# A linear-attention and gated-MLP kernel: issuing from one fixed table instead of by priorities, and short elementwise sums kept in PSUM

## The chip, the cores and the metric

The kernel runs on one core of a Trainium2 chip. TensorE (PE) multiplies matrices into PSUM, of which the kernel uses eight banks; VectorE (DVE), ScalarE (ACT) and GpSimd (POOL) do the elementwise work, POOL on SBUF alone here; SyncE (SP) issues the transfers. Each engine works through its own queue in order and waits on semaphores. The metric is the device time in microseconds (us), the median of the runs.

## What is computed

Three layers follow each other, here as the reference writes them:

```python
for t in range(S):                                   # B=4, H=8, S=768, D=48
    cur = einsum('bhd,bhe->bhde', u * k[t], v[t])
    y[t] = einsum('bhd,bhde->bhe', r[t], state + cur)
    state = w[t][..., None] * state + einsum('bhd,bhe->bhde', k[t], v[t])
x = y, heads side by side                            # 4 x 768 x 384
h = gelu_tanh(x @ w_in); u, v = split(h)             # 512 + 512 columns
v = layernorm(v) * g_ln
v_s = einsum('ts,bsd->btd', w_sg, v) + b_sg
x = x + (u * v_s) @ w_out
gate = sigmoid(causal 5-tap convolution of x over t, one filter per column)
out = (gate * (x @ w_val)) @ w_out2
```

All is float32. Weights of the dense layers arrive as 64-bit numbers and are turned into float32 on ACT and DVE.

## The kernel before

**Attention.** The recurrence runs in chunks of 64 tokens. A unit is one batch, one segment of 256 tokens and one pair of heads: 4 x 3 x 4 = 48 units, 12 to a batch. A unit is a chain of small steps, each a function named by one letter: F and E (L271, L276: prefix products of the decay, DVE scans), L (L280, POOL), K (L283), D (L287, ACT), t (L297, PE transposes), s (L303, PE), k (L307, ACT), m (L311, DVE reads the scores), v (L316, ACT), B (L328 and L333, PE: the products of keys and values), o (L338 ACT and L342 POOL), d (L347, ACT reads what B wrote), a (L353, DVE scan over the chunk states), S and p (L358, L363, ACT), C (L372, PE: the outputs) and y (L377, DVE adds what C wrote to y). One call of the generator `attention(b)` is a tick: it issues different stages of three neighbouring units.

**Dense work.** Tokens of a batch are taken in two halves of 384. Every dense product is made of three passes over fp32r halves (hi and lo of each operand, `PASS` L485), so each operand is first split: ACT copies the hi half, DVE or POOL subtracts to get lo. The steps: xT (L478 PE transposes of y, L481 ACT, L482 DVE), hv (L499 PE, then `ln`: L503 ACT gelu, L505 to L511 DVE with L510 POOL, L514 ACT, L515 POOL), u (PE L522 into `ups`, L535 ACT gelu into `ut`), x2_init (L548 POOL: x again as a sum of its halves), vs (PE L522 into `vps`, 18 matmuls; L562 DVE adds the bias into the SBUF tile `gt`), gated (L573 POOL gt = gt * ut, L575 ACT hi, L576 DVE lo into `gl`), wo (L586 PE, three banks c0 to c2 over four d; then for each bank L597 DVE adds x into the SBUF tile x2, L598 ACT hi and L599 POOL lo of `x2hl`), conv (L615 ACT, L618 four DVE operations, L620 ACT tanh), val (PE L522 into `val`; L631 DVE multiplies by the gate into SBUF, L633 ACT hi, L634 DVE lo into `ml`), out (L644 PE, L650 ACT, L652 the transfer out).

**Order.** Batch 0's attention runs first, together with the decoding of weights (`to_f32`, L150 to L157). Then `phase(b)` walks a list of words (`ORDER0`, `ORDER`, `LAST`), which mixes the dense steps of batch b with ticks T of the attention of batch b+1. That is the program order. The order on each engine is then set by a scheduler: it takes the ready operation of the best priority by its own estimate of times, and the table `LEAD` (L112) moves the priority of each kind of step forward or back. Decoding of w_o1 is held behind batch 0's layer norm with `issue_after` (L743).

**PSUM.** `psA` has three banks (tags a0: t and s, a1: B, a2: C and from batch 1 on xT), `psD` two banks, shared by hv, ups, vps and val (and xT in batch 0), and `psC` three (c0 to c2), which wo, conv and out use in turn, and odd units of batch 0.

Of the kernel before, what the change touches and what calls it, by code (L numbers as in the profile page):

```python
# [25 lines left out]
C = 64  # L26
# [24 lines left out]

@with_exitstack
def tile_kernel(ctx, tc, pk, sv_, rk_, v_, u_, misc_, w_in, w_sgT, b_sg, w_o1, w_val,
                cw, w_o2, ident_, out):
    nc = tc.nc
    pe, act, dve, pool, sp = nc.tensor, nc.scalar, nc.vector, nc.gpsimd, nc.sync
# [10 lines left out]
    psD = ctx.enter_context(tc.tile_pool(name="psD", bufs=2, space=bass.MemoryType.PSUM))  # L67
# [39 lines left out]
    def every(name):  # L107
# [4 lines left out]
    LEAD = {  # L112
# [3 lines left out]
        112, "gate": -97, "wo": -19, "woo": 94, "cv": -371, "val": 38, "out": 2, "outo":  # L116
        203, "dec": 6, "spl": 66, "bon": 100, "du": 177, "dw": -92}

    @contextmanager
    def lead(kind):  # L120
        at = tc.cur_priority
        tc.cur_priority = at - LEAD.get(kind, 0)
        yield
        tc.cur_priority += LEAD.get(kind, 0)

    def leading(kind, f):
        def g(*args):
            with lead(kind):
                return f(*args)
        return g  # L130


    def stage(srcs, ring, tag, words):
# [3 lines left out]
        for src in srcs:  # L137
            n = src.shape[1] * (1 if src.dtype == F32 else 2)
            sp.dma_start(out=big[:, at:at + n], in_=src.bitcast(I32))
# [4 lines left out]
    def to_f32(bits, plain, t):  # L144
# [4 lines left out]
        with lead("dec"):  # L149
# [11 lines left out]
    def split(t, hi, lo):  # L161
        with lead("spl"):
            act.activation(out=hi, in_=t, func=AF.Copy)
            pool.tensor_tensor(out=lo, in0=t, in1=hi.bitcast(F32), op=ALU.subtract)
# [33 lines left out]
    def sg_step(hf, kk):  # L198
# [4 lines left out]
        sp.dma_start(out=t, in_=w_sgT[kk * 128:(kk + 1) * 128, hf * HALF:(hf + 1) * HALF])  # L203
# [9 lines left out]
    def load_nat(b, s):  # L213
        t = r2.tile([128, NT, DM], F32, tag="v", name="v")
        sp.dma_start(out=t, in_=v_[b, s * SEG:(s + 1) * SEG, :].rearrange("(j p) f -> p j f", p=128))
        vt[b, s] = t

    def load_rk(i):
        t = buf("rk", i, i // KS).rearrange("p (two f) -> p two f", two=2)
        sp.dma_start(out=t, in_=rk_[i // KS, i % KS * 128:(i % KS + 1) * 128, :, :])  # L220

    def bonus(b, i):

        s, j = divmod(i, NT)
        with lead("bon"):
# [13 lines left out]
    def load_unit(n):  # L239
        b, s, p = units[n]  # L240
        sp.dma_start(out=buf("pk", n), in_=pk[b, p, s])

    def load_sv(n):
        b, s, p = units[n]
        sp.dma_start(out=buf("sv", n), in_=sv_[b, p, s])

    def unit(n):
# [4 lines left out]
        kh, kn = buf("kh", n), buf("kn", n)  # L252
# [7 lines left out]
        F, E, d1e = buf("F", n), buf("E", n), buf("D1E", n)  # L260
# [62 lines left out]
        def kv():  # L323
            t["b"] = ps(1, n, [128, 512])
# [40 lines left out]
        def tokens():  # L365
            t["c"] = ps(2, n, [128, 512])
# [472 lines left out]
```

## Time and profile before

| | before |
|---|---|
| time, median of 3 runs | 558.68 us (556.5 to 559.03) |
| span of the profiled execution | 554.3 us |
| around the span | 4.4 us, taken as the median less the span |
| PE busy | 520.3 us (94%) |
| DVE busy | 417.0 us (75%) |
| ACT busy | 296.2 us (53%) |
| POOL busy | 267.5 us (48%) |
| mean granted TensorE clock | 0.954 |

The span is the profiled execution's own time from its first instruction to its last; the times include what lies around it. A row of the trace gives an engine, the source line, the tiles as out<-in, a count, busy time and mean duration; "idle before" is time in which the engine sat still before those instructions, with what released it. PE overlaps its matmuls, so the spacing of their starts, as the chain of work shows it, is what a matmul costs there.

### The profile page before, as it was taken

Reading aid. Unit: us, or ns where it says so; the run is one execution under the profiler, and the core shown is the slowest. Engines: PE = TensorE matmul, PEld = TensorE weight load, DVE = VectorE, ACT = ScalarE, POOL = GpSimd, SP = SyncE. Lnnn points to the kernel's source line nnn. Section 1 sums busy time; section 2 is a strip of 40 time slices with the busy share of each in tenths; the row PEclk is TensorE's granted clock in tenths of the full one; section 3 lists DMA queues with packets and bytes.
Section 4 is the critical chain, followed back from the end, with each engine's and each line's share of the span. In section 5 each row is a group of like instructions: output and inputs, shape, how many; then the busy total and the mean of one; then the engine's idle time right before and its main releaser. Section 6 shows DMA issues by size and latency. Waiting matters only on the chain.

```text
span 554.3 us, 10705 instructions
## 1 busy us (share of the span) xinstructions
PE 520.3 (94%) x4060; PEld 448.4 (81%) x4060; DVE 417.0 (75%) x823; ACT 296.2 (53%) x695; POOL 267.5 (48%) x282
## 2 busy tenths in 40 slices
PE   8978688979999999898999999999999999999995
PEld 4666566868988887787988888789989887999985
DVE  6999999899697769985299669965498349324673
ACT  4676856655475745743285746643484636323233
POOL 7477856674844246764154126861163125523430
PEclk9598788896999999999999999999999999999999
DMA  8961513424314343342115342232122100100002
GB/s 302 388 246 44 164 66 103 133 83 158 86 43 138 108 144 100 100 128 90 41 38 178 124 122 72 59 121 80 44 54 91 58 16 1 43 1 0 1 0 86
DMA packets 27075, 53.42 MB, mean 96 GB/s; under 512 B 3089, under 2 KB 17169, under 8 KB 27025
## 3 DMA queue, kind: packets, MB, share of 16 engines
q1 hardware_dynamic: 27024, 52.75, 29.4%
q8 instruction: 32, 0.52, 0.4%
q14 instruction: 19, 0.15, 0.1%
HBM read 48.02 MB, written 4.72 MB: 95 GB/s over the span
## 4 chain that ended last, share of the span: by engine, by line
PE 40%; DVE 16%; issue 3%; DMA 2%; POOL 1%; ACT 1%; POOLq 0%; SPq 0%; ACTq 0%; DVEq 0%
PE vps L522 12%; PE c L586 6%; PE ups L522 6%; PE o L644 4%; DVE cvp L618 4%; PE val L522 3%; PE a L372 3%; PE hv L499 2%; PE a L303 2%; PE a L328 2%; DVE cv L618 1%; PE a L297 1%; DVE SD L353 1%; DVE rk L229 1%; DMA rk<-in_rk_dram 1%
## 5 line engine op out<-in xcount | busy, mean ns | idle before, releaser
L522 PE MATMUL vps<-wsg,vnt 128*128 128x384 f32 x576 | 113.1, 341 | 0.0
L522 PEld LDWEIGHTS vps<-wsg,vnt 128*128 128x128 f32 x576 | 101.1, 190 | 1.0
L573 POOL TENSOR_TENSOR gt<-gt,ut 128x384 f32<-128x384 f32 x32 | 33.8, 1057 | 98.7 <-DVE gt L562 80.5
L499 PE MATMUL hv<-win,x 128*128 128x512 f32 x216 | 65.2, 431 | 3.7 <-DVE cv L631 2.2
L586 PE MATMUL c<-gl,late 128*128 128x384 f32 x288 | 62.6, 345 | 0.0
L522 PE MATMUL ups<-x,win 128*128 128x384 f32 x288 | 59.8, 350 | 1.5 <-DVE gt L562 1.5
L358 ACT ACTIVATE SE<-SD 64x192 f32<-64x192 f32 x80 | 45.1, 564 | 23.1 <-DVE SD L353 13.9
L522 PEld LDWEIGHTS ups<-x,win 128*128 128x128 f32 x288 | 51.4, 192 | 3.0 <-DVE gt L562 1.9
L586 PEld LDWEIGHTS c<-gl,late 128*128 128x128 f32 x288 | 50.2, 189 | 2.2
L499 PEld LDWEIGHTS hv<-win,x 128*128 128x128 f32 x216 | 41.4, 202 | 12.8 <-DVE cv L631 2.6
L280 POOL TENSOR_TENSOR L<-pk,E 128x256 f32<-128x256 f32 x38 | 30.9, 814 | 41.1 <-PE a L372 32.9
L618 DVE SCALAR_TENSOR_TENSOR cvp<-x,cw_col,cvp 128x384 f32<-128x384 f32 x84 | 48.7, 612 | 0.4 <-ACT cvp L615 0.2
L271 DVE TENSOR_TENSOR_SCAN F<-pk,D1F 128x260 f32<-128x260 f32 x40 | 35.3, 884 | 16.5 <-DMA pk<-in_pk_dram 12.3
L353 DVE TENSOR_TENSOR_SCAN SD<-SD,SD 128x288 f32<-128x288 f32 x48 | 43.4, 903 | 4.6 <-ACT SD L347 4.2
L522 PE MATMUL val<-x2hl,late 128*128 128x384 f32 x216 | 44.2, 344 | 2.2 <-ACT vg L503 1.8
L644 PE MATMUL o<-late,ml 128*128 128x384 f32 x216 | 43.9, 342 | 0.7 <-DVE ml L634 0.7
L316 ACT ACTIVATE vcd<-v 64x192 f32<-64x192 f32 x84 | 30.2, 359 | 26.8 <-PE a L328 25.8
L515 POOL TENSOR_TENSOR vnt<-vg,vnt 128x512 fp32r<-128x512 f32 x24 | 34.2, 1426 | 17.9 <-ACT vnt L514 15.3
L576 DVE TENSOR_TENSOR gl<-gt,gl 128x384 fp32r<-128x384 f32 x32 | 20.0, 624 | 29.9 <-ACT gl L575 29.7
L522 PEld LDWEIGHTS val<-x2hl,late 128*128 128x128 f32 x216 | 37.3, 188 | 5.3 <-ACT vg L503 2.7
L575 ACT ACTIVATE gl<-gt 128x384 fp32r<-128x384 f32 x32 | 16.7, 523 | 42.9 <-POOL gt L573 38.2
L644 PEld LDWEIGHTS o<-late,ml 128*128 128x128 f32 x216 | 37.5, 187 | 2.4 <-DVE ml L634 1.0
(154 smaller groups left out, 1102.8 us busy)
## 6 DMA issues: line engine op xcount, KB each, us to landing
pk<-in_pk_dram SPq DMA_DIRECT2D x40, 386.5 KB, 3.4
sv<-in_sv_dram SPq DMA_DIRECT2D x39, 192.0 KB, 2.4
v<-in_v_dram SPq DMA_DIRECT2D x12, 384.0 KB, 3.3
out_dram<-ot SPq DMA_DIRECT2D x24, 192.0 KB, 1.9
rk<-in_rk_dram SPq DMA_DIRECT2D x12, 384.0 KB, 3.1
bits<-in_w_in_dram SPq DMA_DIRECT2D x6, 512.0 KB, 6.8
room_l<-in_pk_dram SPq DMA_DIRECT2D x7, 386.5 KB, 7.1
bits<-in_w_o_dram SPq DMA_DIRECT2D x7, 384.0 KB, 5.3
```

What stands on the lines that cost most here:

```text
L271: dve.tensor_tensor_scan(out=F[:, NW:0:-1], data0=w[:, NW:0:-1], data1=D1F[:, NW:0:-1], initial=0.0, op0=ALU.mult, op1=ALU.add)
L280: pool.tensor_tensor(out=ch(L[:, 0, :]), in0=ch(r), in1=e3[:, :, 0:C], op=ALU.mult)
L316: act.activation(out=vcd[half[c2], :, c2, :], in_=vt[b, s][half[c2], :, 2 * p * D:(2 * p + 2) * D], func=AF.Copy)
L353: dve.tensor_tensor_scan(out=SD1, data0=SD1, data1=SD0, initial=0.0, op0=ALU.add, op1=ALU.mult)
L358: act.activation(out=S[half[hh], :, hh, :], func=AF.Copy, in_=d1[half[hh], :, 1:NC + 1].rearrange("p e c -> p c e"))
L499: pe.matmul(out=ps, lhsT=x[:, a, kk, j * 128:(j + 1) * 128], rhs=win[:, w, kk, DV:2 * DV], start=(z == 0), stop=(z == nmm - 1))
L515: pool.tensor_tensor(out=vnt[b][:, 1, i, :], in0=vg, in1=hi.bitcast(F32), op=ALU.subtract)]
L522: pe.matmul(out=ps, lhsT=lhs(a, kk), rhs=rhs(w, kk), start=(z == 0), stop=(z == nk * 3 - 1))
L573: pool.tensor_tensor(out=t, in0=t, in1=ut.pop((b, hf, d)), op=ALU.mult)
L586: pe.matmul(out=acc[0][f], lhsT=late["wo1"][:, a, d, f * 128:(f + 1) * 128], rhs=g[:, w, :], start=(d == 0 and q == 0), stop=(d == KV - 1 ...
L618: dve.scalar_tensor_tensor(out=t, in0=x2[:, f, k:k + HALF], scalar=cw_col[:, f, k:k + 1], in1=t, op0=ALU.mult, op1=ALU.add)
L644: pe.matmul(out=acc2[0][j], lhsT=m[:, a, j * 128:(j + 1) * 128], rhs=late["wo2"][:, w, g, :], start=(g == 0 and q == 0), stop=(g == KD - 1 ...
```

## The change

All engine calls of the program are no longer issued where the functions make them. An engine is now a `Queue` that writes each call into a log under the word of its step (kind and running number), and at the end one loop issues all of them, in the order of the table `SCHEDULE`, with the scheduler off. A step is cut into pieces: three instructions for the dense matmul steps and `ln`, one or two for most elementwise steps, up to 16 for the attention's matmuls. `LEAD` and `issue_after` are gone. The words of `ORDER0`, `ORDER` and `LAST` change in a few places. Beside that, five things change in what is computed where:

- `psD` has three banks and `psA` two. B of unit n+1 and C of unit n share one bank, the tile `bc` (batches 1 to 3); xT and C of even units of batch 0 move to `psD`.
- The gate product goes from POOL to DVE, 32 operations. In 29 of them vso (the bias) and the gate are written over the product `vps` in PSUM, and hi and lo are read from there; in 3 they stay in `gt`.
- The residual sum is written over the bank c, hi and lo are made from there, lo on DVE where it was on POOL (24), and ACT copies the sum to the SBUF tile x2 (24 new operations).
- The product of gate and val is written over the bank `val`, and hi and lo are read from there.
- wo, out, x2_init and the rows of out are steps of their own for each bank.

The diff, cut (of the table the first and the last line):

```diff
+SIZE = dict.fromkeys(("hv", "u", "vs", "wo", "val", "out", "ln"), 3)
+SIZE.update(dict.fromkeys("FvS", 2), z=2)
+SCHEDULE = """
+pk0 z0 zp4 pk1 ld0 ld1 nat0 pk2 zp0 pk3 wl0 wps0 zp7 zp5 zp1 zp3 a0 zp8 zp11 zp2 F0 wl2 D0 K0 E0 wl1
...
+valo22 out65 valo22 out66 valo23*2 out69 out68 outo21 out67 outo21 out71 out70 outo22*2 outo23*2"""
...
-    pe, act, dve, pool, sp = nc.tensor, nc.scalar, nc.vector, nc.gpsimd, nc.sync
+    log, counts, here = [], {}, ["x"]
+    class Queue:
+        def __init__(self, engine):
+            self.engine = engine
+        def __getattr__(self, op):
+            f = getattr(self.engine, op)
+            return lambda *a, **k: log.append((here[-1], self, f, a, k))
+    pe, act, dve, pool, sp = (Queue(e) for e in (nc.tensor, nc.scalar, nc.vector, nc.gpsimd, nc.sync))
...
-    psD = ctx.enter_context(tc.tile_pool(name="psD", bufs=2, space=bass.MemoryType.PSUM))
+    psD = ctx.enter_context(tc.tile_pool(name="psD", bufs=3, space=bass.MemoryType.PSUM))
...
         def kv():
-            t["b"] = ps(1, n, [128, 512])
+            t["b"] = shared(n)[:, 2 * NT * D:] if not first else ps(1, n, [128, 512])
...
         def tokens():
-            t["c"] = ps(2, n, [128, 512])
+            t["c"] = shared(n + 1)[:, 0:2 * NT * D] if not first else ps(2, n, [128, 512])
...
+    VISIT = "C2 B1 y2 d1 a1 S1 p1 t0 s0 k0 m0 v0"
+    both = {}
+    def shared(n):
+        if n not in both:
+            both[n] = psA.tile([128, 512], F32, tag="a1", name="bc")
+        return both[n]
     def ps(i, n, shape):
+        if i == 2 and n % 2 == 0:
+            return psD.tile(shape, F32, tag="d", name="a2")
...
-        ring, tag = (psD, "d") if b == 0 else (psA, "a2")
-        a = ring.tile([128, KD, 128], F32, tag=tag, name="a4")
+        a = psD.tile([128, KD, 128], F32, tag="d", name="a4")
...
-        t = rgt.tile([128, HALF], F32, tag="t", name="gt")
+        t = ps if (b, hf, d) in ut else rgt.tile([128, HALF], F32, tag="t", name="gt")
...
-            pool.tensor_tensor(out=t, in0=t, in1=ut.pop((b, hf, d)), op=ALU.mult)
+            dve.tensor_tensor(out=t, in0=t, in1=ut.pop((b, hf, d)), op=ALU.mult)
...
-                    dve.tensor_tensor(out=xx, in0=acc[0][f], in1=xx, op=ALU.add)
-                    act.activation(out=hl[:, 0, f, :], in_=xx, func=AF.Copy)
-                    pool.tensor_tensor(out=hl[:, 1, f, :], in0=xx, in1=hl[:, 0, f, :].bitcast(F32),
-                                       op=ALU.subtract)
+                    a = acc[0][f]
+                    dve.tensor_tensor(out=a, in0=a, in1=xx, op=ALU.add)
+                    act.activation(out=hl[:, 0, f, :], in_=a, func=AF.Copy)
+                    dve.tensor_tensor(out=hl[:, 1, f, :], in0=a, in1=hl[:, 0, f, :].bitcast(F32),
+                                      op=ALU.subtract)
+                    with step("x2"):
+                        act.activation(out=xx, in_=a, func=AF.Copy)
...
-            dve.scalar_tensor_tensor(out=t, in0=t, scalar=1.0, in1=ps, op0=ALU.add, op1=ALU.mult)
+            dve.scalar_tensor_tensor(out=ps, in0=t, scalar=1.0, in1=ps, op0=ALU.add, op1=ALU.mult)
+            t = ps
...
+    with tc.manual_schedule():
+        for word in SCHEDULE.split():
+            word, _, times = word.partition("*")
+            for _ in range(int(times or 1)):
+                for f, a, k in parts[word].pop(0):
+                    f(*a, **k)
```

How instructions stand on the engines, at three places. L930 is the issuing loop, the line of every instruction after the change.

PE, where the first spatial-gating product `vps` meets the last units of batch 1's attention, before (`a` is a bank of psA, `SE`, `sv` and `L` are C's operands):

```order
L328 MATMUL a_1573<-vcd_119,kn_111 64x96 x4
L333 MATMUL a_1573<-misc,rk_120 128x2 x2
L522 MATMUL ups<-x,win 128x384 x9
L297 MATMUL a_1589<-ident,kh_106 128x128 x2
L522 MATMUL vps<-wsg_613,vnt 128x384 x14
L372 MATMUL a_1563<-SE_121,L_103 64x96
L522 MATMUL vps<-wsg_613,vnt 128x384
L372 MATMUL a_1563<-sv_104,L_103 64x96
```

and at the first `vps` after the change:

```order
L930 MATMUL hv<-win,x 128x512 x3
L930 MATMUL a_273<-L_103,kh_106 64x64 x8
L930 MATMUL vps<-wsg_171,vnt 128x384 x3
L930 MATMUL ups<-x,win 128x384 x3
L930 MATMUL a_273<-ident,kh_106 128x128 x2
L930 MATMUL vps<-wsg_171,vnt 128x384 x6
L930 MATMUL ups<-x,win 128x384 x3
L930 MATMUL vps<-wsg_171,vnt 128x384 x3
```

Before, the whole product `ups` comes first and the matmuls L372 of a unit's outputs stand one by one between those of `vps`; after, products of u and vs alternate in threes, between pieces of the attention that are whole.

DVE at the same place before (`spare` and `bits` are the decoding of weights, `y` the sum that frees the bank of L372):

```order
L273 RECIPROCAL D1E_112<-F_108 128x4
L155 SCALAR_TENSOR_TENSOR spare<-bits,spare 128x384 x2
L157 SCALAR_TENSOR_TENSOR spare<-bits,spare 128x384 x2
L151 TENSOR_SCALAR spare<-spare 128x384
L153 TENSOR_SCALAR spare<-spare 128x384
L155 SCALAR_TENSOR_TENSOR spare<-bits,spare 128x384
L377 TENSOR_TENSOR y<-a_1563,y 128x2x96
L157 SCALAR_TENSOR_TENSOR spare<-bits,spare 128x384
L562 SCALAR_TENSOR_TENSOR gt<-vps,misc,b_bc 128x384 x2
```

and after, at its first bias operation:

```order
L930 SCALAR_TENSOR_TENSOR spare<-bits,spare 128x384 x4
L930 SCALAR_TENSOR_TENSOR gt<-vps,misc,b_bc 128x384
L930 SCALAR_TENSOR_TENSOR vps<-vps,misc,b_bc 128x384
L930 TENSOR_TENSOR vps<-vps,ut 128x384
L930 TENSOR_TENSOR L_101<-a_282,misc 128x256
L930 SCALAR_TENSOR_TENSOR vps<-vps,misc,b_bc 128x384
L930 SCALAR_TENSOR_TENSOR SD_117<-SD_117,SD_113 128x288
L930 TENSOR_TENSOR gl<-vps,gl 128x384
L930 TENSOR_SCALAR spare<-spare 128x384
L930 TENSOR_TENSOR y<-bc,y 128x2x96
L930 TENSOR_SCALAR spare<-spare 128x384
L930 TENSOR_TENSOR vps<-vps,ut 128x384
```

Before, seven operations of decoding stand ahead of y, and the bias operations behind it; after, bias, gate and lo operations have moved ahead of much of the decoding, and one operation of it stands right ahead of y.

PE in the ticks of batch 3's attention beside batch 2's second products, before:

```order
L328 MATMUL a_4739<-vcd_119,kn_111 64x96 x2
L297 MATMUL a_4748<-ident,kh_107 128x128
L328 MATMUL a_4739<-vcd_119,kn_111 64x96
L297 MATMUL a_4748<-ident,kh_107 128x128
L328 MATMUL a_4739<-vcd_119,kn_111 64x96
L303 MATMUL a_4748<-L_101,kh_107 64x64 x8
L644 MATMUL o_4692<-late,ml 128x384 x3
L644 MATMUL o_4693<-late,ml 128x384 x3
L644 MATMUL o_4694<-late,ml 128x384 x3
```

and after, where products of the same kinds stand:

```order
L930 MATMUL a_635<-L_102,kh_107 64x64 x8
L930 MATMUL val<-x2hl,late 128x384 x3
L930 MATMUL vps<-wsg_269,vnt 128x384 x6
L930 MATMUL o_645<-late,ml 128x384 x3
L930 MATMUL vps<-wsg_269,vnt 128x384 x6
L930 MATMUL a_635<-ident,kh_107 128x128 x2
L930 MATMUL vps<-wsg_269,vnt 128x384 x3
L930 MATMUL val<-x2hl,late 128x384 x6
L930 MATMUL o_647<-late,ml 128x384 x3
```

Before, B (L328), the transposes (L297) and the scores (L303) of a tick alternate; after, the pieces of a tick stand together (scores, transposes), and pieces of `val`, `vps` and `o` alternate in threes between them.

## Rows read from the trace of the kernel before

**Rows 1.** The page: busy us of each engine, share of the span, instructions.

```profile
PE 520.3 (94%) x4060; PEld 448.4 (81%) x4060; DVE 417.0 (75%) x823; ACT 296.2 (53%) x695; POOL 267.5 (48%) x282
```

**Rows 2.** Stretches: length, busy us of PE, PEld, DVE, ACT, POOL, clock, transfers.

```profile
0.00:152.00 152.00, 131.65 (x1091) 102.52 (x1092) 136.68 (x260) 92.55 (x229) 100.53 (x113) 0.84 0.48 162
152.00:210.00 58.00, 58.00 (x528) 51.08 (x527) 46.92 (x98) 33.59 (x84) 24.91 (x28) 1.00 0.35 107
...
400.00:457.00 57.00, 56.98 (x501) 49.50 (x501) 38.33 (x78) 33.68 (x78) 18.61 (x19) 1.00 0.17 53
...
533.00:554.00 21.00, 14.82 (x80) 13.53 (x79) 12.68 (x22) 8.86 (x19) 3.74 (x3) 0.94 0.15 57
...
125.00:135.00 10.00, 9.50 (x47) 8.64 (x48) 9.41 (x18) 4.82 (x13) 5.49 (x5) 0.50 0.68 218
```

**Rows 3.** Waits of PE over the run: us in total, times, longest.

```profile
PE a L372 <- DVE y L377: 4.2, 1, 4.2
...
PE hv L499 <- DVE cv L631: 2.2, 2, 1.3
PE val L522 <- ACT vg L503: 1.8, 2, 1.1
...
PE ups L522 <- DVE gt L562: 1.5, 1, 1.5
```

**Rows 4.** Timeline around 125 us, DVE, then PE: start, us, instructions.

```profile
125.01 0.35 DVE L377 TENSOR_TENSOR y<-a,y 128x192 f32<-128x192 f32 x1
...
125.50 0.59 PE L372 MATMUL a<-SE,L 128*64 128x96 f32 x4 [4.19 <-DVE y L377]
```

**Rows 5.** The chain of work from 386 to 413 us: start, us, what.

```profile
390.93 0.86 PE a L372 x16
391.79 1.78 PE ups L522 x9
393.57 1.56 PE c L586 x9
395.13 1.58 PE ups L522 x9
396.71 0.47 PE a L328 x6
397.18 0.26 PE a L297
397.44 0.31 PE a L328 x2
397.75 0.26 PE a L297
...
409.40 0.48 PE a L328 x8
...
412.38 0.22 PE a L297 x2
```

**Rows 6.** DVE's groups from 60 to 80 us (two lines), from 380 to 400 us (one).

```profile
L353 DVE TENSOR_TENSOR_SCAN SD<-SD,SD 128x288 f32<-128x288 f32 x3 | 3.2, 1076 | 0.0
...
L482 DVE TENSOR_TENSOR x<-a,x 128x384 fp32r<-128x384 f32 x2 | 1.1, 542 | 0.0
...
L353 DVE TENSOR_TENSOR_SCAN SD<-SD,SD 128x288 f32<-128x288 f32 x2 | 1.5, 754 | 1.1 <-ACT SD L347 1.1
```

**Rows 7.** Groups of POOL, DVE and ACT over the run: busy us, mean ns, idle before.

```profile
L573 POOL TENSOR_TENSOR gt<-gt,ut 128x384 f32<-128x384 f32 x32 | 33.8, 1057 | 98.7 <-DVE gt L562 80.5 <-ACT SD L287 7.8 <-ACT ut L535 6.2
...
L599 POOL TENSOR_TENSOR x2hl<-x,x2hl 128x384 fp32r<-128x384 f32 x24 | 25.5, 1076 | 25.8 <-ACT x2hl L598 25.8
...
L576 DVE TENSOR_TENSOR gl<-gt,gl 128x384 fp32r<-128x384 f32 x32 | 20.0, 624 | 29.9 <-ACT gl L575 29.7
...
L597 DVE TENSOR_TENSOR x<-c,x 128x384 f32<-128x384 f32 x24 | 12.6, 549 | 4.9 <-PE c L586 4.6
...
L481 ACT ACTIVATE x<-a 128x384 fp32r<-128x384 f32 x24 | 11.6, 485 | 5.9 <-PE a L478 5.8
```

More of the change, by code (lines that the diff above doesn't have):

```diff
@@ L108, in every, with step, stepping @@
         return parts[name][0]
-    LEAD = {
[3 rows of a table removed]
-        112, "gate": -97, "wo": -19, "woo": 94, "cv": -371, "val": 38, "out": 2, "outo":
-        203, "dec": 6, "spl": 66, "bon": 100, "du": 177, "dw": -92}
     @contextmanager
-    def lead(kind):
-        at = tc.cur_priority
-        tc.cur_priority = at - LEAD.get(kind, 0)
+    def step(kind):
+        counts[kind] = counts.get(kind, -1) + 1
+        here.append(f"{kind}{counts[kind]}")
         yield
-        tc.cur_priority += LEAD.get(kind, 0)
-    def leading(kind, f):
+        here.pop()
+    def stepping(kind, f):
         def g(*args):
-            with lead(kind):
+            with step(kind):
                 return f(*args)
@@ L453, in attention @@
         for n in range(n0, n1 + 2):
-            for i in (2, 1, 0):
-                step(n - i, STAGES[i + 1])
-                if i == 1 and b < SUMMED:
-                    step(n - i, "o")
+            for w in VISIT.split():
+                go(n - int(w[1:]), w[0])
+            if b < SUMMED:
+                go(n - 1, "o")
             run_loads("sv", n - 1)
@@ L546, in x2_init @@
                 dve.tensor_copy(x2[:, :, 0:TAPS - 1], halo)
-            for f in range(KD):
+        for f in range(KD):
+            with step("ix"):
                 pool.tensor_tensor(out=x2[:, f, TAPS - 1:], in0=x[:, 0, f, :].bitcast(F32),
@@ L582, in wo_step @@
             acc[0] = [psC.tile([128, HALF], F32, tag=f"c{f}", name=f"c{f}") for f in range(KD)]
-        with lead("wo"):
-            for f in range(KD):
+        for f in range(KD):
+            with step("wo"):
                 for q, (a, w) in enumerate(PASS):
@@ L640, in out_step @@
             acc2[0] = [psC.tile([128, DM], F32, tag=f"c{f}", name=f"o{f}") for f in range(KD)]
-        with lead("out"):
-            for j in range(3):
+        for j in range(3):
+            with step("out"):
                 for q, (a, w) in enumerate(PASS):
@@ L646, in out_step @@
         if g == KD - 1:
-            with lead("outo"):
-                for j in range(3):
+            for j in range(3):
+                with step("outo"):
                     t = rgt.tile([128, DM], F32, tag="t", name="ot")
@@ L716, in first_loads @@
             elif c in small:
-                sp.dma_start(out=small[c][0], in_=small[c][1])
+                with step("ld"):
+                    sp.dma_start(out=small[c][0], in_=small[c][1])
             elif c == "W":
@@ L762, in tile_kernel @@
         phase(b)
+    parts, last = {}, {}
+    for word, q, *call in log:
+        l = parts.setdefault(word, [])
+        most = SIZE.get(word.rstrip("0123456789"), 16 if q is pe else 1)
+        if not l or last[word] is not q or len(l[-1]) >= most:
+            l.append([])
+        l[-1].append(call)
+        last[word] = q
+    with tc.manual_schedule():
[4 more added lines that the diff above has]
+                    f(*a, **k)
+    assert not any(parts.values())
 def pack(r, k, w):
```

254 lines of the change are left out of this document (190 added, 64 removed), and 3 rows, old and new, of the table LEAD.

## Prediction

> **What bounds the kernel now.** I read the busy times first, then the stretches, then PE's own waits, and the chain of work last. On the page PE is busy 94% and DVE 75% [rows 1]. The stretches show two kernels in one [rows 2]. Up to 152 us, while batch 0's attention runs alone and weights are decoded, PE is busy 131.65 us at a mean clock of 0.84, and DVE 136.68 us: DVE is the one that leads there. From 152 us on PE is full: 58.00 of 58 us, 56.98 of 57, at full clock, and DVE has air (46.92 and 38.33). So a change of elementwise work pays in the first part if it takes DVE off the path, and in the second part only as far as PE gets denser or loses a wait. Of waits PE has few [rows 3]: the longest is one of 4.2 us behind a y on DVE, and three kinds that are waits for a free PSUM bank of psD (hv behind the reader of `val`, val behind the reader of `hv`, ups behind the reader of `vps`) make 2.2 + 1.8 + 1.5 = 5.5 us. PE's list names neither POOL nor a transfer.
>
> **Part 1, the first 152 us.** At 121 us PE has its outputs L372 ready to go, but the bank is freed by a y, and y stands on DVE behind decoding of weights (the order of DVE above); y starts at 125.01, L372 at 125.50 after 4.19 us [rows 4]. Behind the hole PE runs ten microseconds at half its clock: from 125 to 135 us the granted clock is 0.50, the lower of the two levels [rows 2]. After the change less decoding stands ahead of the bias and y operations. Going through DVE's order in both kernels with the mean duration of each kind (in all the 136.68 us of its 260 instructions in this stretch [rows 2]), the DVE work ahead of the first bias operation is 110.4 us where it was 114.5, thus 4.1 less, about the wait itself. Against this, this part also takes four gates and three lo operations on DVE, 7 x 0.549 = 3.8 us [rows 7] (L597 is the nearest kind: one input in PSUM, one in SBUF, same size), which stand behind the first products, where PE has other work. I take -4.1, with ends at +3.8 (the wait stays and the new work is on the path) and -9.1 (the wait goes, and the ten microseconds at half clock, which came behind a PE that stood still, take five).
>
> **Part 2, changes of work on PE.** The chain shows what interrupting costs [rows 5]. The nine matmuls of c that follow those of ups take 1.56 us, the ups after them 1.58; the ups that follows the attention's L372 takes 1.78. So each return from attention to dense work costs 0.20 us, and a change between dense products costs nothing. Within the attention, B and the transposes cut into each other take 0.47 + 0.26 + 0.31 + 0.26 = 1.30 us, and apart 0.48 + 0.22 = 0.70: 0.30 for each of two added changes. Counted over PE's order in both kernels, returns to dense work are 113 before and 83 after; from the end of batch 0's first half on, where PE is the bound, 84 and 63. That is 21 x 0.20 = 4.2 us. Changes within the attention there go from 107 to 84; 23 of them cost between nothing and 0.30 each, and as most are not of the kind in the row, I take 0.10: 2.3 us. The third place in the order above shows both. Matmuls themselves are the same in number and size. Part 2: -6.5, with ends at 0 (the price is paid elsewhere, by a later wait) and -11.1 (4.2 + 6.9).
>
> **Part 3, PSUM banks.** psD goes from two banks to three, which speaks for the 5.5 us of bank waits going. But the banks are held longer. Before, `vps` is free after one bias operation; now the bank stays until bias, gate, ACT's hi and DVE's lo are done. And xT comes to psD as well, while B and C share a bank. In the order, the places where less than 1 us of PE's work lies between the last reader of a bank and its next writer are 13 before and 20 after. The 13 cost 5.5 us, 0.42 each; seven more make +3.0. Ends: -5.5 (all gone) and +9.1 (each of the seven at 1.3 us, the longest single wait for hv).
>
> **Part 4, work moved between engines.** POOL loses 32 gates and 24 lo operations, 33.8 + 25.5 = 59.3 us [rows 7]. Nobody on PE's list waited for them, so their going alone is worth nothing to PE. DVE gets 56 operations at 0.549 us, 30.7 us. It gets something back: the scan L353, both inputs in SBUF, takes 1076 ns where POOL is at work and 754 where it rests, while L482, with one input in PSUM, takes 542 in the crowded stretch [rows 6], no more than the like L597's 549 over the run [rows 7]. So a microsecond of POOL is worth up to 322/1076 = 0.30 of DVE: at most 17.8 us, and as DVE is busy three quarters of the time and not all its operations are of that kind, I take 10. DVE then has 417 + 31 - 10 = 438 us, 79%, below PE in the whole, and I take the cost as nothing beyond part 3. If that cover is gone it is the first rival. ACT gets 24 copies at 0.485 (L481) [rows 7], 11.6 us on 296; only the convolution waits for them, and val has the half's other products over it. If the cover fails, it is one copy a half, 8 x 0.485 = 3.9 us.
>
> The Trainium skill has a rule here, in SBUF — State Buffer, section Who interferes with whom: a DVE operation with two SBUF inputs and a POOL operation that reads SBUF exclude each other for a whole instruction. The direction agrees with L353 and L482 above. Were every one of the 56 POOL operations to hold up DVE for half of its 1.06 us, 30 us of DVE would come back instead of 10, and the third rival is what that would give.
>
> **Part 5, the end.** The last 21 us hold the last convolution and out; DVE is busy 12.68 of them [rows 2], with the twelve convolution operations in one row. Three lo operations (1.6 us) now stand on DVE and three copies (1.5 us) on ACT ahead of it, in part beside the products that still run. I take +0.5, ends 0 and +3.1.
>
> **Sum.** -4.1 - 6.5 + 3.0 + 0.5 = -7.1. The span of 554.3 becomes 547.2; with the 4.4 us around it 551.6 us, against a median of 558.68. From here on 0.5%, that is 2.8 us, is the least that a measurement of this kernel can tell from no change.
>
> **Rivals.** *One, slower: DVE waits for ACT, in order.* Each split on DVE waits for ACT's hi: L576 stood idle 29.7 us over 32 such, 0.93 each [rows 7]. The change adds 24 such lo operations, and 13 of the 36 y on shared banks wait for ACT to have read its columns of the bank, which none did before: 37 x 0.93 = 34 us in which DVE stands, with F, E and a of the next tick behind. Where it decides: from 152 to 210 us DVE has 46.92 of 58 us [rows 2]; 14 new operations (8 gates at most, 6 lo) make 54.6, and an eighth of the 34 makes 58.9. There PE starts to wait. If half of the 34 us reach PE, the time is 551.6 + 17 = 568.6; from 7 us on, a fifth, the gain is gone. Against it: DVE also stood for these 29.7 us before, and only 5.5 us of anything reached PE through banks. The Trainium skill, PSUM — Partial Sum Buffer, section PSUM bank collisions raise a hardware error, says that two engines on one bank and partition quadrant are to be ordered by semaphores even where both only read; that is why y and d of two units on one `bc` wait for each other, and speaks against sharing it. No row of before shows such a wait.
>
> *Two, no change: gains are given back.* PE gets denser, but the bank waits go to their upper end: 558.7 - 4.1 - 6.5 + 9.1 + 0.5 = 557.7. For it: PE is at 94% and the longer holding is certain. It includes the case that a saved return only ends in the next wait.
>
> *Three, a larger gain.* DVE becomes so much freer that the first part gives its 9.1 us, and the third bank saves all 5.5 us: 558.7 - 9.1 - 6.5 - 5.5 = 537.6. For it: DVE bounds the first part. Against it: POOL's gates are few there.
>
> That the table only repeats the old order is ruled out by the counts of part 2.
>
> **Chances.** The forecast, 541 to 555.9: 0.50. Three, below 541: 0.14. Two, within 0.5%: 0.18. One, above 561.5: 0.18. Faster 0.64, same 0.18, slower 0.18. The range goes from 537 to 567: it leaves out about 0.04 below and 0.14 above.
>
> **What would show it.** Part 1: PE's hole at 121 us gone, batch 0's first c products ending at about 148 instead of 152 us. Part 2: PE's busy time falling by about 6 us or more, with the same matmuls, and nine dense matmuls at 1.6 us more often than at 1.8. Part 3: PE's waits for readers in DVE at 8 or 9 us in all after 150 us. Part 4: POOL near 208 us, DVE between 430 and 448, L353 at about 754 ns in more stretches. Rival one: y and x2hl on DVE waiting for ACT by tens of us, and PE waiting for y, L or bank readers by over 10 us in the middle of the run. The forecast is wrong if PE's idle time after 152 us grows by more than its busy time falls.

## The result

The changed kernel takes 525.32 us (523.87 to 527.37, four runs) where the kernel before, on the same chip, takes 557.59: a ratio of 0.9436, with a 95% interval of 0.9396 to 0.9475. It is faster by 32 us, or 5.6%. The forecast was 551.6, in a range from 537 to 567: the direction was right, the size a quarter of what came, and the time lies 12 us below the range.

The page of the kernel after has these busy times, to be read against [rows 1]:

```profile
PE 494.8 (95%) x4060; PEld 435.5 (83%) x4060; DVE 414.2 (79%) x879; ACT 301.2 (58%) x719; POOL 197.9 (38%) x226
```

PE does the same 4060 matmuls in 25.5 us less. DVE has 56 operations more and is 2.8 us less busy. The span goes from 554.3 to 523.5 us, by 30.8. Where it went is best read at the ends of the wo products (the start of the last matmul on c of each half), which both kernels pass in the same sequence:

| from, to | before, us | after, us | difference |
|---|---|---|---|
| start to the end of the first half's c | 152.6 | 143.3 | -9.3 |
| second half (the rest of batch 0) | 58.1 | 58.1 | 0.0 |
| third and fourth (batch 1) | 68.2 + 56.4 | 64.1 + 48.6 | -11.9 |
| fifth and sixth (batch 2) | 65.1 + 56.4 | 58.0 + 56.7 | -6.8 |
| seventh and eighth (batch 3) | 52.5 + 23.3 | 50.1 + 23.2 | -2.5 |
| to the last matmul | 16.0 | 17.1 | +1.1 |
| to the end of the span | 5.7 | 4.3 | -1.4 |

So a third of the gain is in the first part, and two thirds lie where PE was full already [rows 2], all but 2.5 us of it while the attention of the next batch runs beside the dense work.

**The first part.** The stretch to the first half's end and the 27 us ahead of it, of the kernel after (length, busy us of PE, PEld, DVE, ACT, POOL, granted clock, transfers):

```profile
0.00:143.00 143.00, 123.22 (x1101) 95.54 (x1102) 121.27 (x256) 90.21 (x224) 88.36 (x104) 0.88 0.48 162
...
116.00:143.00 27.00, 25.50 (x213) 23.70 (x212) 23.68 (x50) 17.99 (x47) 17.61 (x17) 1.00 0.39 125
```

DVE is busy 121.27 us where it was 136.68 [rows 2], with about as many instructions. PE's wait of 4.2 us for y [rows 3, 4] is gone, and the granted clock is 1.00 in the last 27 us, where before it was 0.50 for ten of them [rows 2]. But PE stands still in this part as long as before, 143.00 - 123.22 = 19.8 us against 152.00 - 131.65 = 20.4. What fell is its busy time, and with it the time at the lower clock: with levels of 1.00 and 0.50, means of 0.84 and 0.88 make 49 us at half clock before and 34 after. The changes of tile (explained below) fall here too, from 115 to 89.

**The part in which PE is full.** PE's waits after, over the whole run (us, times, longest):

```profile
PE a L930 <- ACT room_w L930: 5.0, 2, 2.8
...
PE bc L930 <- ACT SE L930: 1.2, 4, 0.4
...
PE vps L930 <- DVE gt L930: 0.7, 1, 0.7
PE a L930 <- DVE gl L930: 0.6, 1, 0.6
...
PE ups L930 <- DVE gl L930: 0.4, 1, 0.4
```

The first is in the first part. The waits for a reader of a psD bank are down to 0.7 + 0.6 + 0.4, with one of 0.2 more: 1.9 us where [rows 3] have 5.5. That is a small part of what PE saved. The larger part shows in the distance from one matmul's start to the next. Here is the timeline of one tick, first of the kernel before (start, us, instructions):

```profile
424.18 0.39 PE L372 MATMUL a<-SE,L 128*64 128x96 f32 x4
...
424.89 0.39 PE L328 MATMUL a<-vcd,kn 128*64 128x96 f32 x4
425.20 0.33 PE L297 MATMUL a<-ident,kh 128*128 128x128 f32 x1
425.46 0.38 PE L328 MATMUL a<-vcd,kn 128*64 128x96 f32 x2
425.77 0.33 PE L297 MATMUL a<-ident,kh 128*128 128x128 f32 x1
426.03 0.38 PE L328 MATMUL a<-vcd,kn 128*64 128x96 f32 x2
426.34 0.68 PE L303 MATMUL a<-L,kh 64*64 64x64 f32 x16
426.95 1.85 PE L644 MATMUL o<-late,ml 128*128 128x384 f32 x9
```

and of the kernel after:

```profile
372.27 0.55 PE L930 MATMUL bc<-vcd,kn 128*64 128x96 f32 x8
372.65 0.39 PE L930 MATMUL bc<-SE,L 128*64 128x96 f32 x4
...
373.46 0.68 PE L930 MATMUL a<-L,kh 64*64 64x64 f32 x16
374.08 0.79 PE L930 MATMUL vps<-wsg,vnt 128*128 128x384 f32 x3
...
389.86 1.21 PE L930 MATMUL vps<-wsg,vnt 128*128 128x384 f32 x6
390.90 0.38 PE L930 MATMUL a<-ident,kh 128*128 128x128 f32 x2
391.04 0.77 PE L930 MATMUL vps<-wsg,vnt 128*128 128x384 f32 x3
```

The figure with a star is the tile of the PE array that a matmul uses: 128*128 for all dense products and for transposes, 128*64 for B and C, 64*64 for the scores. Before, the transposes L297 cut B in three, and each cut changes the tile twice: from 424.89 to 426.34 the eight matmuls of B and two transposes take 1.45 us. After, B takes 0.38 us, C follows in the same tile, and the attention's transposes stand between dense products (390.90), where two of them take 0.14 us and nothing else. I took the distance of every matmul's start to the next from the end of the first half's c to the last matmul, took off the usual distance of its kind in a row (0.174 us for 384 columns, 0.233 for hv, 0.042 and 0.041 for B and C, 0.0315 for a score, 0.107 for a transpose), and sorted what is left by the kind of the next matmul:

| left over beyond the usual distance, us | before | after |
|---|---|---|
| at changes to, from and within the attention | 22.7 | 10.0 |
| in waits of over 0.3 us | 9.7 (10) | 7.0 (14) |
| inside runs of one attention kind | 6.9 | 3.0 |
| inside and between dense products | 10.5 | 10.9 |
| usual distances | 345.7 | 344.6 |
| sum, PE from there on | 395.3 | 375.5 |

By pairs, what is left over has its median at 0.094 us from a dense product to B, C or s, at 0.135 from B or C to a dense product or a transpose, at 0.117 from s to any other, at 0.09 to 0.15 from a transpose to B, C or s, at 0.00 from B to C, from a dense product to a transpose, and from one dense product to another (in before; in after B to C is 0.03, and in both a transpose ahead of a dense product is 0.08 shorter than its usual distance). So what costs in these pairs is a change of tile. From the first half's end on before has 205 such changes and after 104.

### The profile page after: what moved, and what is told of

Read it like the earlier page. It is cut to its first block, busy times and chain, and to the rows that moved or that the text cites. A ratio compares the mean times of both kernels' runs of the same rounds, so it can differ in the third digit from the quotient of the medians.

```text
span 523.5 us, 10670 instructions
## 1 busy us (share of the span) xinstructions
PE 494.8 (95%) x4060; PEld 435.5 (83%) x4060; DVE 414.2 (79%) x879; ACT 301.2 (58%) x719; POOL 197.9 (38%) x226
## 5 line engine op out<-in xcount | busy, mean ns | idle before, releaser
L930 PE MATMUL vps<-wsg,vnt 128*128 128x384 f32 x576 | 119.2, 341 | 2.1 <-DVE gt L930 0.7
L930 PEld LDWEIGHTS vps<-wsg,vnt 128*128 128x128 f32 x576 | 100.0, 188 | 4.7 <-DVE gt L930 1.0
L930 POOL TENSOR_TENSOR L<-pk,E 128x256 f32<-128x256 f32 x38 | 30.3, 797 | 103.7 <-DVE E L930 41.4
L930 PE MATMUL hv<-win,x 128*128 128x512 f32 x216 | 62.0, 417 | 1.9 <-ACT x L930 1.4
L930 PE MATMUL ups<-x,win 128*128 128x384 f32 x288 | 62.9, 342 | 0.4 <-DVE gl L930 0.4
L930 PE MATMUL c<-gl,late 128*128 128x384 f32 x288 | 60.6, 339 | 0.0
L930 PEld LDWEIGHTS ups<-x,win 128*128 128x128 f32 x288 | 50.9, 188 | 1.5 <-DVE gl L930 0.5
L930 PEld LDWEIGHTS c<-gl,late 128*128 128x128 f32 x288 | 50.3, 188 | 1.5 <-DVE gl L930 0.4
L930 ACT ACTIVATE SE<-SD 64x192 f32<-64x192 f32 x80 | 45.0, 562 | 10.5 <-DVE SD L930 9.8
L930 DVE SCALAR_TENSOR_TENSOR cvp<-x,cw_col,cvp 128x384 f32<-128x384 f32 x84 | 49.8, 613 | 0.4
L930 PEld LDWEIGHTS hv<-win,x 128*128 128x128 f32 x216 | 40.1, 195 | 10.4 <-DVE x L930 2.0
L930 PE MATMUL o<-late,ml 128*128 128x384 f32 x216 | 47.9, 343 | 0.4 <-ACT ml L930 0.2
L930 POOL TENSOR_TENSOR vnt<-vg,vnt 128x512 fp32r<-128x512 f32 x24 | 33.8, 1415 | 33.4 <-ACT vnt L930 33.4
L930 PE MATMUL val<-x2hl,late 128*128 128x384 f32 x216 | 45.8, 344 | 0.0
L930 POOL TENSOR_TENSOR x<-x 128x384 f32<-128x384 f32 x24 | 27.1, 1135 | 48.9 <-DVE cvp L930 44.5
L930 DVE TENSOR_TENSOR_SCAN SD<-SD,SD 128x288 f32<-128x288 f32 x48 | 38.1, 795 | 8.0 <-ACT SD L930 7.6
L930 PEld LDWEIGHTS o<-late,ml 128*128 128x128 f32 x216 | 37.6, 188 | 3.3 <-DVE ml L930 1.3
L930 PEld LDWEIGHTS val<-x2hl,late 128*128 128x128 f32 x216 | 37.2, 188 | 1.9 <-DVE ml L930 0.5
L930 DVE SCALAR_TENSOR_TENSOR vps<-vps,misc,b_bc 128x384 f32<-128x384 f32 x29 | 17.9, 619 | 22.4 <-PE vps L930 22.4
L930 ACT ACTIVATE gl<-vps 128x384 fp32r<-128x384 f32 x29 | 14.2, 489 | 36.9 <-DVE vps L930 31.8
L930 DVE TENSOR_TENSOR_SCAN F<-pk,D1F 128x260 f32<-128x260 f32 x40 | 30.7, 767 | 3.3 <-DMA pk<-in_pk_dram 3.0
L930 ACT ACTIVATE vcd<-v 64x192 f32<-64x192 f32 x84 | 30.1, 358 | 5.0 <-PE bc L930 2.6
```

What stands on the lines that cost most here:

```text
L930: f(*a, **k)
```

## The experiments

Theory A was that the table's order carries the gain, since it halves the changes of tile on PE. The rivals: B, the operands in PSUM and POOL's lighter load carry it, by a faster DVE; C, the third bank does. Where the table below gives a time, it is a median of four runs or more; "changes" are changes of tile on PE after the first half, "at changes" and "waits" are the first two lines of the table above.

| kernel | time, us | changes | at changes, us | waits, us | PE from the first half on, us |
|---|---|---|---|---|---|
| before | 557.6 | 205 | 22.7 | 9.7 | 395.3 |
| after | 525.3 | 104 | 10.0 | 7.0 | 375.5 |
| m1_no_table | 580.3 | 165 | 16.7 | 31.6 | 420.9 |
| m2_banks_only | 575.2 | 144 | 15.4 | 33.6 | 421.9 |
| m3_operands_only | 596.6 | 207 | 24.7 | 33.0 | 430.4 |
| s3_more_changes | 531.8 | 135 | 13.7 | 6.1 | 380.7 |
| n1_before_179 | 560.6 | 179 | 19.6 | 13.9 | 397.4 |
| n2_before_165 | 571.9 | 164 | 17.5 | 24.4 | 406.2 |
| n3_before_224 | 576.9 | 223 | 25.7 | 19.6 | 412.7 |

### The change without its table

m1 is the kernel before with the banks, the shared bank, the operand moves and the new words, ordered by the scheduler and LEAD; m2 has the banks only (with xT and the shared bank as in the change), m3 the operand moves only (the residual sum and the value product as in the change). m1 and m2 also have the change's order of stages within a tick. On the kernel before, of m2:

```diff
-    psD = ctx.enter_context(tc.tile_pool(name="psD", bufs=2, space=bass.MemoryType.PSUM))
+    psD = ctx.enter_context(tc.tile_pool(name="psD", bufs=3, space=bass.MemoryType.PSUM))
```

and of m3:

```diff
-        t = rgt.tile([128, HALF], F32, tag="t", name="gt")
+        t = ps if (b, hf, d) in ut else rgt.tile([128, HALF], F32, tag="t", name="gt")
...
-            pool.tensor_tensor(out=t, in0=t, in1=ut.pop((b, hf, d)), op=ALU.mult)
+            dve.tensor_tensor(out=t, in0=t, in1=ut.pop((b, hf, d)), op=ALU.mult)
```

> Everything of the change but the fixed table: banks, bank sharing, operand moves and the new words, ordered by the scheduler with LEAD as before. Theory A (the table's order on PE carries the gain: a matmul of one tile shape behind one of another costs 0.12 us, and the table has half as many such changes): from the end of the first half on this kernel has 165 changes of shape on PE where before has 205 and after 104, so PE gains 40 x 0.115 = 4.6 us there, the first part gains little; time 545 to 556 us. Theory B (the operands in PSUM and POOL's lighter load carry it): nearly all of the gain is here, 525 to 532 us.

> Before, with only the third bank for psD, the shared bank for B and C, and xT in psD, ordered by the scheduler. Theory A: 145 changes of shape after the first half instead of 205, 60 x 0.115 = 6.9 us, so about 550 us. Theory C (bank waits carry the gain, 5.5 us of them in the profile of before): about 552 us, and the waits of ups, val and hv for readers are gone. Theory B: 557.

> Before, with only the operand moves: gate on DVE in PSUM, residual sum in PSUM with lo on DVE and a copy to x2 on ACT, value product in PSUM; two banks for psD, ordered by the scheduler. Theory A: 207 changes of shape, no gain on PE; banks held longer with only two of them; 555 to 566 us. Theory B: DVE gets about 20 us back from POOL and 54 fewer waits between engines: 530 to 545 us.

Measured: 580.34 (ratio 1.0419, interval 1.0387 to 1.0452), 575.20 (1.0329, 1.0297 to 1.0362) and 596.63 us (1.0693, 1.0632 to 1.0754). All three are slower than before. B and C fall: neither the operands nor the banks bring anything by themselves in the scheduler's order, and in m2 PE still waits 2.2 and 2.1 us for readers of psD's three banks (vps for `gt`, val for `vg`). Theory A's numbers fall too; the changes of tile cost what it said (16.7 and 15.4 us), but PE waits three times as long. PE's and DVE's longest new waits in m1:

```profile
PE a L297 <- DVE L L311: 16.8, 7, 4.5
...
DVE F L271 <- ACT SD L287: 17.2, 19, 1.8
DVE y L377 <- PE bc L328: 11.0, 11, 2.7
```

The first wait is as long in m2 (16.8 us in 7 places) and m3 (16.4 in 10), where before has 4.5 us in 5, so it comes with the banks alone and with the operands alone; why stays open. The last line is the shared bank: y, in order on DVE, waits for the B of the next unit, which writes to the same bank after C. And a PE that stands still pays twice. The granted clock of after, m1 and m3 in 40 slices, in that order:

```profile
PEclk9679699899999999999999999999999999999999
```
```profile
PEclk9699589979889998999997999799989998999999
```
```profile
PEclk9897688967996999699998999799989997999999
```

In after the clock is full from a quarter of the span on; in m1 and m3 it falls again and again. In m1 it is at half six times after the first half, 34 us in all, each time within 2 us of the end of a PE wait of 1.3 to 3.4 us (other waits of that size had no such fall); its mean from 152 to 573 us is 0.96. LEAD's numbers were those of the kernel before, so m5 changed the one that the longest wait points to:

```diff
-        145, "m": -188, "v": 80, "o": 91, "d": -23, "a": 2, "S": 58, "p": -174, "C":
+        145, "m": 0, "v": 80, "o": 91, "d": -23, "a": 2, "S": 58, "p": -174, "C":
```

> Everything of the change but the fixed table, as in m1, with one number of LEAD changed: the masked scores m (DVE, L311) get 0 instead of -188. In m1 PE waits 16.8 us in 7 places for that operation before the next transposes. Theory L (the priorities, set for the old operands and banks, are what makes the change slower without the table): most of the 16.8 us go, and the time falls from 580 to about 562 to 568 us. Rival (the new operands and banks themselves are slower): within 5 us of 580.

Measured: 579.78 us (1.0407, 1.0361 to 1.0452), and the wait is still there with 17.4 us in 7 places. Theory L falls in this form. Whether some other set of priorities would give the scheduler a good order for the new operands stays open.

### Only the changes of tile

s1 and s2 put one small matmul ahead of each product ups, vps and val of the kernel after, 88 in all, one in a 64*64 tile and one, as the control, in the full tile.

```diff
+            nc.tensor.matmul(out=ps[64:128, 0:64], lhsT=ident[0:64, 0:64], rhs=ident[0:64, 0:64], start=True, stop=True)
```

and in s2

```diff
+            nc.tensor.matmul(out=ps[:, 0:64], lhsT=ident, rhs=ident[:, 0:64], start=True, stop=True)
```

> After, with one extra matmul of 64x64x64 written into the bank ahead of each product ups, vps and val (88 of them; what it writes is overwritten). Each makes two changes of tile shape in a row of full-size matmuls. Theory A (a change of shape costs 0.09 to 0.13 us): 88 x (0.094 + 0.117 + 0.06 of its own) = 24 us more than after, about 549 us. Rival (a short matmul costs its own time and no more): 88 x 0.06 = 5 us, about 531 us, less than with a full-shape extra.

> The control: the same 88 places, with an extra matmul of the full shape (128 rows, 128 columns, 64 moving). Theory A: no change of shape, 88 x 0.11 us of its own (half a transpose of 128 columns, which takes 0.107 for each of its two passes) = 9 us, about 535 us. Rival: as much or more than the 64x64 one, since it is the larger matmul.

Measured: 550.71 and 539.19 us, 25.4 and 13.9 more than after. The matmul with a quarter of the work costs nearly twice as much. The same place in both, between two rows of ups, s1 and then s2:

```profile
257.11 0.69 PE L939 MATMUL ups<-x,win 128*128 128x384 f32 x3
257.73 0.33 PE L666 MATMUL ups<-ident 64*64 64x64 f32 x2
257.98 0.44 PE L667 MATMUL ups<-x,win 128*128 128x384 f32 x1
258.26 0.52 PE L939 MATMUL ups<-x,win 128*128 128x384 f32 x2
```
```profile
258.16 0.69 PE L939 MATMUL ups<-x,win 128*128 128x384 f32 x3
258.69 0.33 PE L666 MATMUL ups<-ident 128*128 128x64 f32 x2
258.83 0.42 PE L667 MATMUL ups<-x,win 128*128 128x384 f32 x1
259.09 0.51 PE L939 MATMUL ups<-x,win 128*128 128x384 f32 x2
```

From the first start to the last it is 1.15 us in s1 and 0.93 in s2; over the 61 such places after 150 us the difference is 0.20 us in the mean, for two changes of tile. The rival, a short matmul's own time and no more, falls. The control cost 5 us more than its 9: an extra of the full tile adds 0.23 us in the rows above (0.93 us from the first start to the last, in which four matmuls of ups would take 0.70), twice the 0.11 that was expected, while PE's waits of over 0.3 us fall from 7.0 to 1.7.

s3 moves 20 dense pieces of the table a few places, so that they stand between B and C or between C and s (one of them below); nothing else differs.

```diff
-B25 xTo11 C24
+B25 xTo11 val4 C24
```

> After, with 20 dense pieces of the table moved by one or a few places so that they stand between B and C or between C and the scores: 135 changes of shape on PE after the first half where after has 104, everything else as it is. Theory A: 31 x 0.115 = 3.6 us more, about 529 us. Rival: no difference, 525 us.

Measured: 531.78 us (0.9515, 0.9473 to 0.9557), 6.5 more than after. What is left over at changes rises by 3.7 us, as 31 x 0.115 says; PE in all needs 5.2 more, in a profiled execution that was the fastest of the six (527.18). The rival, no difference, falls by little: the intervals of s3 and after just touch (0.9473 and 0.9475). The first part ended at 140.0 us in this profile, against 143.3 in after: the kernels of this study that share this first part, but for a few operations, lie between 140.0 and 147.0 us there.

n1, n2 and n3 change the count in the kernel before, by one or three priorities. In n1 B gets 60 (it had none, that is 0):

```diff
-        145, "m": -188, "v": 80, "o": 91, "d": -23, "a": 2, "S": 58, "p": -174, "C":
+        145, "m": -188, "v": 80, "o": 91, "B": 60, "d": -23, "a": 2, "S": 58, "p": -174, "C":
```

In n2 B gets 50, and s and C go from -7 and 104 to 50; in n3 s goes from -7 to -60.

> Before, with one priority added for B (60 ahead, nothing else): 179 changes of tile shape on PE after the first half instead of 205. Theory A: PE loses 26 x 0.115 = 3.0 us there and, if no wait takes their place, the time falls to about 554.5 us. Rival (what the table does for the waits and the clock carries the gain, not the shapes): the spacings at changes fall by 3 us, but the time moves with PE's waits, either way.

> Before, with B, C and s at one priority (50): 165 changes instead of 205. Theory A: 40 x 0.115 = 4.6 us less, about 553 us. Rival: as in n1; the fewer changes the scheduler's order has, the longer PE may wait for operands that come in bunches.

> Before, with the scores s later (-60 instead of -7): 224 changes instead of 205. Theory A: 19 x 0.115 = 2.2 us more, about 560 us. Rival: as in n1.

Measured: 560.59 (1.0033, 1.0017 to 1.0050), 571.87 (1.0237, 1.0215 to 1.0259) and 576.94 us (1.0337, 1.0314 to 1.0360). What is left over at changes follows the count as forecast: -3.1, -5.2 and +3.0 us, where 3.0, 4.6 and 2.2 were expected. The time does not: the waits are 13.9, 24.4 and 19.6 us where before has 9.7, and the time follows the sum of both (33.5, 41.9 and 45.3 us, before 32.4), with a granted clock of 0.99, 0.98 and 0.98 from 150 to 540 us where before has 1.00. n2's tile changes fall by a fifth and it is 14 us slower. So the count of changes explains 12.7 us of the gain, and is worth that only in an order that makes PE wait no more than before. The table does both. No run has a fixed table for the old banks and operands, so what the third bank and the shared one are worth under a table is not shown.

### The operand moves under the table

m4 puts the residual sum back into SBUF with its lo half on POOL, m6 the value product back into SBUF, m7 both. p1 leaves all as in after and adds as much POOL work as was taken away. The gate was not put back on POOL in any run, so its share stays open.

Of m4, on the kernel after:

```diff
-                    dve.tensor_tensor(out=a, in0=a, in1=xx, op=ALU.add)
+                    dve.tensor_tensor(out=xx, in0=a, in1=xx, op=ALU.add)
...
-                    dve.tensor_tensor(out=hl[:, 1, f, :], in0=a, in1=hl[:, 0, f, :].bitcast(F32),
+                    pool.tensor_tensor(out=hl[:, 1, f, :], in0=xx, in1=hl[:, 0, f, :].bitcast(F32),
```

of m6:

```diff
-            dve.scalar_tensor_tensor(out=ps, in0=t, scalar=1.0, in1=ps, op0=ALU.add, op1=ALU.mult)
-            t = ps
+            dve.scalar_tensor_tensor(out=t, in0=t, scalar=1.0, in1=ps, op0=ALU.add, op1=ALU.mult)
```

and of p1, once with each gate and twice with each lo half of the residual sum:

```diff
+                nc.gpsimd.tensor_tensor(out=dump, in0=b_bc[:, 0:288], in1=b_bc[:, 0:288], op=ALU.mult)
```

> After, with the residual sum back in SBUF, its lo half on POOL (24 operations of 1.08 us) and no copy to x2; the table's order otherwise. Theory A: shape changes stay at 104, so within 3 us of after, 523 to 529 us. Theory B: the 25 us of POOL work come back with 7 us or more of slower DVE operations and the longer chain to val: 530 to 540 us.

> After, with only the product of gate and value back in SBUF (its bank is free after one DVE operation, its lo half reads two SBUF tiles). If holding a bank of psD longer costs PE time: 2 us or more faster than after. If reading SBUF twice beside POOL costs DVE time that PE feels: 2 us or more slower. Forecast: within 2 us of after, 523 to 528 us.

> After, with both the residual sum with its lo half on POOL and the value product back in SBUF: of the operand moves only the gate stays. Theory A (the order carries the gain): within 3 us of m4, 527 to 533 us, so most of the gain of 32 us is still there. Theory B: 540 us or more.

> After, with 80 extra POOL operations (128x288, two inputs in SBUF, output to a tile nobody reads; one with each gate and two with each lo half of the residual sum), as much POOL work as the change took away. Theory B (POOL's lighter load speeds DVE and so the kernel): DVE's busy time rises by 20 us or more, the time by 5 us or more. Theory A: DVE's busy time may rise, but the time stays within 3 us of after.

Measured: m4 530.16 (0.9527, 0.9468 to 0.9586), m6 525.72 (0.9449, 0.9394 to 0.9503), m7 531.15 (0.9525, 0.9474 to 0.9576), p1 533.64 us (0.9552, 0.9505 to 0.9600). The value product's place makes no difference, so a bank of psD held through three more operations costs nothing here. The residual sum is worth about 5 us, little more than the noise in m4 alone, but m7 repeats it. By the number m4 falls in theory B's range, not in A's. POOL's load costs 8 us: p1's time is theory B's, though DVE's busy time rose by 7.7 us and not by 20. In p1 PE's waits of over 0.3 us after the first half are 13.2 us where after has 7.0, among them 1.9 for an operand that POOL itself makes (`wsg`; after has 0.6). Busy times of m4 and p1:

```profile
PE 500.9 (94%) x4060; PEld 439.4 (83%) x4060; DVE 414.5 (78%) x855; ACT 292.3 (55%) x695; POOL 222.2 (42%) x250
```
```profile
PE 494.1 (93%) x4060; PEld 434.5 (82%) x4060; DVE 421.9 (80%) x879; ACT 301.3 (57%) x719; POOL 258.8 (49%) x306
```

m4 has 24 DVE operations fewer than after, 13 us at 0.55, and DVE is as busy: 24 us more POOL work made the rest of DVE 13 us slower. In p1 61 us more made it 7.7 us slower, less for each us; its extra operations are issued beside DVE's gates and lo halves, which have an operand in PSUM; that this is the reason was not tested. m7 keeps of the operand moves only the gate, and 26 of the 32 us are still there.

v1 took 24 normalisations of the layer norm from DVE to ACT:

```diff
-            dve.tensor_scalar(out=vg, in0=vg, scalar1=mv[:, 0:1], scalar2=rs, op0=ALU.subtract,
-                              op1=ALU.mult)
+            dve.scalar_tensor_tensor(out=nb, in0=mv[:, 0:1], scalar=-1.0, in1=rs, op0=ALU.mult, op1=ALU.mult)
+            act.activation(out=vg, in_=vg, func=AF.Identity, scale=rs, bias=nb)
```

> After, with the normalisation of the layer norm (24 DVE operations of 128x512, about 0.65 us) on ACT as one operation with scale and bias, and a 128x1 operation on DVE that makes the bias: DVE loses 24 x (0.65 - 0.15) = 12 us, ACT gains about 24 x 0.6 = 15. If DVE still sets the pace of the first part or of the middle: 3 to 8 us faster than after, about 519 us. If DVE is no longer what bounds any part (Theory A: PE's order does): within 2 us of after, 523 to 528 us.

Measured: 530.06 us (0.9514, 0.9481 to 0.9547), 4.7 slower than after: DVE is 9.2 us less busy (405.0), and that brings nothing any more. PE's waits of over 0.3 us after the first half rise from 7.0 to 10.7 us, of which 2.0 are for ACT's `vg`. No version tried beats the kernel after.

## Why the prediction was wrong

**Part 2 is the step that failed.** It counted returns from attention to dense work (84 to 63) at 0.20 us and changes within the attention at 0.10, 6.5 us in all. The prices read from [rows 5] were of the right size. L372 to ups is 128*64 to 128*128, 0.135 us by the starts there, with 0.095 on the way in from ups to L372 that was not counted; a transpose that cuts B changes the tile twice, 0.135 + 0.152. But the class was wrong. What costs is a change of tile, 0.09 to 0.15 us each: 205 before and 104 after, and what is left over at changes falls by 12.7 us, nearly twice the forecast. A return from a transpose costs nothing, and the table puts most of the attention's transposes beside dense products: 24 of 30 runs of them stand right ahead of one, where before 6 of 41 did. A step from B to C costs next to nothing, and the shared bank comes with an order in which 19 of 32 runs of C follow B directly, where 8 of 44 did. Runs of one attention kind lost another 3.9 us, which the working did not have. The tile stands in each row of PE's timeline, and was there to be counted.

The Trainium skill states this class, in TensorEngine Tiling (Array Packing), section Key Properties: "Changing tiling mode (not just tile) drains the TensorE". The traces agree, with the 0.20 us for two changes between s1 and s2 beside it; the page gives no price.

**Part 1** named a wait that did go, and the first part fell by 9.3 us, where -4.1 was taken and -9.1 was the far end. But that the number came near the far end is in part luck. The hole of 4.2 us behind y is gone, and other waits took its place: PE stands still there for 19.8 us, as it did for 20.4. What is gone is time at half clock, 49 us against 34, worth about 7 us by an estimate (half of the difference), and 26 changes of tile, which the working counted only behind the first half. What DVE does there became 15 us shorter, which was not expected at all. In the kernels that share this first part it ends at 140.0 us with 24 us at half clock (s3) and at 147.0 with 44 (s2), so part of the 9.3 us belongs to the execution that was profiled. m2 with the banks alone has the first half's end at 146.3, and the share of table and banks there stays open.

**Part 3** had the wrong sign: +3.0 was expected, and the waits for readers of psD fell from 5.5 to 1.9 us. The count of places with less than 1 us between reader and writer (13 to 20) said nothing on waits, and m6 shows that the longer holding is covered.

**Part 4.** POOL came out at 197.9 for 208, DVE at 414.2 for 438. The relief was taken as 10 us and was 33. The DVE scan over the chunk states, over the run, before and after, beside [rows 6]:

```profile
L353 DVE TENSOR_TENSOR_SCAN SD<-SD,SD 128x288 f32<-128x288 f32 x48 | 43.4, 903 | 4.6 <-ACT SD L347 4.2
...
L930 DVE TENSOR_TENSOR_SCAN SD<-SD,SD 128x288 f32<-128x288 f32 x48 | 38.1, 795 | 8.0 <-ACT SD L930 7.6
```

Its mean of 795 ns is near the 754 without POOL. Some of the relief is of a kind that the working had no term for: in m6 the lo halves of the value product take 644 ns from two SBUF tiles, in after 550 with one operand in PSUM, and POOL is as busy in both. The estimate of 30 us beside the rule on DVE and POOL in the prediction was nearer than the 10 that was taken from the rows, but p1 does not bear it out as a price: with 61 us of POOL work back DVE is 7.7 us slower. And "worth nothing to PE" was 5 to 8 us short, by m4 and p1.

**Part 5**, +0.5, came out at +1.1 to the last matmul and -1.4 behind it.

**The sum.** The span was forecast at 547.2 us and was 523.5. Of the 23.7 us between, part 2 is 10.1 (12.7 + 3.9 - 6.5), part 3 is 5.7 (+3.0 against -2.7 in waits of over 0.3 us), part 1 is 5.2. Another 2.6 us is the time around the span, 4.4 in the forecast and 1.8 in the profiled execution of after (525.27 - 523.5). In other executions of before it is about 2 us (556.15 and 554.1 beside n1), so a median less the span of another execution overstated it.

**The rivals.** The first, DVE waiting for ACT, did not come in the kernel after; its lo halves of the gate wait less than before [rows 7]:

```profile
DVE gl L930 <- ACT gl L930: 7.4, 14, 1.1
...
DVE y L930 <- ACT SD L930: 5.2, 6, 1.6
```

Without the table the time does go beyond the 568.6 of that rival, m1 to m3 lie between 575 and 597 us, and DVE does wait for ACT in m1 and m2 (F for SD, 17.2 us in each, where before has 3.9). But PE's longest wait in all three is for the masked scores, and y waits for PE rather than for ACT (11.0 us for B in m1). The third, a larger gain, was the nearest, with 537.6 at a chance of 0.14, and it lacks the 10 us by which part 2 fell short.

## What to carry to other kernels

Count the changes of PE tile in an order before pricing it, not the changes of work: here each cost 0.09 to 0.15 us, and transposes placed beside full-size products were free. An order with fewer of them pays only if PE does not wait more for it, and a kernel's operands, banks and order are one design: moving the operands or the banks under an order made for others cost 18 to 40 us, and with an order of their own they were part of a gain of 32, in which 26 us were left with two of the operand moves taken back (m7).

## What the runs showed that was not expected

The cost of a stall on PE is larger than the stall: in m1 PE's waits after the first half grew by 22 us, and PE needed 25.6 us more although its changes of tile cost 6 us less, with a granted clock of 0.96 where the kernel after has 1.00. And the price of POOL's work to DVE was 0.55 us for each us in m4 and 0.13 in p1; what makes the difference was not tested.
